# Seven half-size products in a sixth FFN tile too, weight sums made in two other tiles, last batch's plain q copied by DMA

## The chip, the core and the metric

The kernel runs on one core of one Trainium2 chip. The metric is the device time of one execution in microseconds (us), taken as the median of several runs. The engines are named as in the profile: PE is TensorE's matmuls, PEld its weight loads, DVE is VectorE, ACT is ScalarE, POOL is GpSimd, and SP is SyncE, whose queue issues DMAs.

## What is computed

Attention over 8 batches of 576 tokens with 8 heads of 64, then a feed-forward layer on the 4608 tokens of 512 that come out:

```
scores = q @ k^T / 8,  masked:
    heads 0 to 3 (plain):    0 <= i - j < 32
    heads 4 to 7 (dilated):  0 <= i - j < 128 and (i - j) % 4 == 0
x   = softmax(scores) @ v            # (8, 576, 8 x 64) -> (4608, 512)
h   = max(x @ w_in, 0)               # (4608, 2048)
out = (h * h) @ w_out                # (4608, 512), float32
```

Matrix products are in bfloat16 and accumulate in float32 in PSUM.

## The kernel before, in words

**Tiles and groups.** The feed-forward layer goes over nine tiles of 512 tokens, counted from one in this document (the first two tiles are worked on as four halves). Each tile is a list of 32 groups of instructions, so the n-th tile has the groups 32(n-1) to 32(n-1)+31. The first 16 are its first layer: group u multiplies x by 128 columns of w_in into one PSUM bank `pf` (L986, 4 matmuls of 512 columns), ScalarE takes the maximum with zero into `h2T` (L999), and VectorE squares it there (L1002). The other 16 are the second layer.

**The second layer, plain** (`g2`, L1157; tiles one to six). For each of four blocks of 128 tokens, 16 matmuls of 512 columns add into one bank (L1165), four in each group; ScalarE copies the bank to `osb` (L1171), and SP's queue stores it (L950).

**The second layer by seven products** (`g2_fast`, L1111; tiles seven to nine, `fast`, from `FAST * NT` tokens on). The 2048 inner rows are cut into two halves, the tokens of the tile into two halves, and the 512 output columns into two halves. Instead of eight products of half size, seven are made (M1 to M7, table `PRODUCTS` at L1093), each of 16 matmuls with 256 columns: 8 values of f times 2 blocks of tokens i. They need sums of the parts of h (`add_up`, L1032, four VectorE operations for a range of f, into `h_sum`, which lies in the staging buffers `rb[2]`, and in place in `h2T`) and sums of the parts of w_out (`weigh`, L1263, eight VectorE operations of 128x1024, into `w_sum`, which lies in `rb[0]`). The four quarters of the result, c11, c12, c21 and c22, lie in one buffer `whole`; `after` (L1057) copies a bank into a quarter on ScalarE or adds a bank to one on VectorE (`plus`, L1049), and `keep` (L1052) stores. In these tiles two f's that belong together are squared by one operation of 1024 elements, except the last two. f=0 to 7 (the low half) come from the even u, f=8 to 15 from the odd u. `sums_at` (L1024) says after which u the sums are made: 7, 11 and 15. Where an attention visit follows the first layer (`visited`, only the seventh tile), two of the last four sums are put off to a step of their own, "Z0".

Order before: M1 into bank X, M5 into Y, M6 on top of M1 in X, M3 on top of M5 in Y, M7 on top in X, M2 into Z, M4 on top in X. `after` reads the bank between the products that grow in it.

**The attention around it.** The attention of batch b (0 to 7) is spread over the groups as steps: (group number, order within a group, batch, code). `natural_step` (L696) carries one out after the group with that number is issued:

- "V": a visit (`quadrants`, L381): TensorE makes the scores of up to two heads' pairs e of a batch and the weighted sums of two others, all 64x64 quadrant matmuls (L376). Scores go to two banks `pa`, or to two banks `pf` for a second pair; sums and denominators to `po` and `pd`, and to two `pf` for a second pair.
- "E": exponential on ScalarE (L742), mask on VectorE (L747) and small sums there (L750, L759). A code with "e" makes only the exponentials, one with "m" only the masks.
- "L" and "X": the logarithm of the denominator (L709, L710), its exponential (L724) on ScalarE, and two multiplications on VectorE (L727, and L731 for 16 tokens whose values stand in a bank `pa`) that write x.
- "R", "K", "Q": `arrange` (L333) copies the transposed q and k of a batch into the layouts that the visits read (L352 and L355 for R, L346 for K, L344 for Q), mostly on VectorE.

From the sixth batch (b = 5) on, batch b has visits behind the groups 32(b-1)+15 and 32(b-1)+23, that is, between the first and second layer of tile b, counted from one, and in the middle of its second layer. In the sixth tile the first visit is that of b = 6; the second one makes scores of b = 7 and sums of b = 6. R of batch 7 stands at the groups 167 to 170, K at 170 to 172 and 184 to 187, Q at 173 to 175 and 188 to 191. In the third tile, R of batch 4 stands at the groups 82 to 85, and a visit behind group 88.

**What sets the order.** The program is written in the order in which each engine is to run it; every engine takes its own instructions strictly in that order, and waits are put in where two engines use the same tile. The main loop is:

```
    for g, group in enumerate(groups):
        ...
        group()
        if G * (FAST - 1) < g <= G * (FAST - 1) + 8:
            weigh(g - G * (FAST - 1) - 1)
        ...
        while steps and steps[0][0] <= g:
            natural_step(*steps.pop(0)[2:])
```

So before, the eight `weigh` operations stand behind the groups 161 to 168, in the sixth tile's first layer; a `weigh` stands ahead of the steps of its group. PSUM banks `pf` are four, given out in turn; `pa` are two; `po` and `pd` one each.

Of the kernel before, what the change touches and what calls it, by code (L numbers as in the profile page):

```python
# [63 lines left out]
def kernel(  # L64
# [9 lines left out]
    nc = tc.nc  # L74
    P = nc.NUM_PARTITIONS
    B, H, S, D = q.shape
# [17 lines left out]
    NT = 512  # L94
    NTILES = NTOK // NT
    XB = 2
    FAST = 6
    PAIRED = 5
    STAGE = (0, 1, 0, 2, 1, 1, 1, 1)
    NATURAL = 3  # L100
# [232 lines left out]
    def arrange(b: int, what: str, g: int, jj: int, e=None, copy=nc.vector.tensor_copy):  # L333

        src, rows = sides[jj], sides[g]
        n = H // 2
        hs = slice(0, n) if e is None else slice(2 * e, 2 * e + 2)  # L340
        if what == "Q" and b == XB:
            copy(qT[rows, 0:2, jj::2, :], qx[b % 2][src, g:4:2, :, :])
        elif what == "Q":
            copy(q_both[rows, hs, jj::2, :], qx[b % 2][src, hs, :, :])  # L344
        elif what == "K":
            nc.vector.tensor_copy(  # L346
                k_both[rows, g::2, hs, :].rearrange("p i h (c j m) -> p j (h c) i m", c=2, j=2)[:, jj, :, :, :],
                kx[b % 2][src, hs, :, :].rearrange("p h c (i m) -> p (h c) i m", m=16)[:, :, g::2, :],
            )
        else:  # L350
            ms = (slice(128, M), slice(0, 16))[g]
            copy(  # L352
                ends[b % 2][rows, 0, :, :].rearrange("p h (r m) -> p h r m", r=RES)[:, :, jj::2, :], qx[b % 2][src, n:, :, ms]
            )
            copy(  # L355
                ends[b % 2][rows, 1, :, :].rearrange("p h (m c j) -> p j h c m", c=2, j=2)[:, jj, :, :, :],
                kx[b % 2][src, n:, :, ms],
            )
# [337 lines left out]
    def natural_step(b: int, code: str):  # L696
        what, e = code[0], int(code[1])
        if what == "Z":
            late.pop()()
        elif what in "QKR":  # L700
            arrange(b, what, e, int(code[2]), *(int(x) for x in code[3:4]), *[nc.scalar.copy][: len(code) - 4])
        elif what == "V":
            scs, pvs = ([(int(x[0]), int(x[1])) for x in y.split(",") if x] for y in code[2:].split("/"))
            quadrants(scs, pvs)
        elif what == "L":
            _, d, rest = op[b, e]
            rec = recs[b, e] = r_pool.tile([P, 576], f32, name="rec")
            if rest[0][0] is rest[0][1]:
                nc.scalar.activation(rec[:, 0:512], d[:, :], ACT.Ln)  # L709
                nc.scalar.activation(rec[:, 512:576], rest[1][0], ACT.Ln)  # L710
            elif rest[0][0] is not rest[1][0]:
                nc.scalar.activation(rec[:, 0:512], d[:, :], ACT.Ln)
                for g in range(2):
                    to = sides[g ^ crossed(b, e)]
                    nc.scalar.activation(rec[to, 512:576], rest[1][g][to, :], ACT.Ln)
            else:
                for g in range(2):
                    to, at = sides[g], sides[1 - g]
                    nc.scalar.activation(rec[to, 512:576], rest[1][g][at, :], ACT.Ln)
                    nc.scalar.activation(rec[to, 0:512], d[at, :], ACT.Ln)  # L720
        elif what == "X":
            o, _, rest = op.pop((b, e))
            rec = recs.pop((b, e))
            nc.scalar.activation(rec[:, :], rec[:, :], ACT.Exp, scale=-1.0)  # L724
            t0 = b * M % (RING // RES)
            tok = xT[:, e, :, t0 : t0 + M]
            nc.vector.tensor_tensor(out=tok[:, :, 16:M], in0=byr(o[:, :]), in1=byr(rec[:, 0:512]), op=ALU.mult)  # L727
            for g, rows in enumerate(sides) if rest[0][0] is not rest[0][1] else [(0, slice(0, P))]:
                if rest[0][0] is not rest[1][0]:
                    g = g ^ crossed(b, e)  # L730
                nc.vector.tensor_tensor(  # L731
                    out=tok[rows, :, 0:16], in0=byr(rest[0][g][rows, :]), in1=byr(rec[rows, 512:576]), op=ALU.mult
                )
        else:
            g = int(code[2])
            second = g ^ ((b, e) in ((NATURAL, 1), (B - 1, 1)))
            n = 384 if e >= NE // 2 else (448, 384)[g]
            if "m" not in code:
                if not second:
                    pts[b, e] = p_pool.tile([P, 896], bf16, name="pt")  # L740
                pt = pts[b, e][:, 448 * g : 448 * g + n]
                nc.scalar.activation(pt, sp[b, e][g][:, 0:n], ACT.Exp, scale=SCALE)  # L742
            if "e" in code:
                return
            pt = pts[b, e][:, 448 * g : 448 * g + n]
            mask = (mask_f if e >= NE // 2 else mask_p[:, 384:] if b == XB else mask_n)[:, 0:n]
            nc.vector.tensor_tensor(out=pt, in0=pt, in1=mask, op=ALU.mult)  # L747
            if second and e >= NE // 2 and b > XB:
                z = pts[b, e][:, :].rearrange("p (x y) -> p x y", x=2)[:, :, 0:320].rearrange("p x (c m) -> p x c m", c=2)
                nc.vector.tensor_tensor(  # L750
                    out=shared[:, e - NE // 2], in0=z[:, :, :, 48:80], in1=z[:, :, :, 80:112], op=ALU.add
                )
            if second and e < NE // 2:
                even, odd = (
                    pts[b, e][:, y : y + 384].rearrange("p (i r m) -> p i r m", i=4, r=RES) for y in (0, 448)
                )
                for x, one, two in ((0, even, odd), (1, odd[:, 0:3], even[:, 1:4])):
                    n = 4 - x
                    nc.vector.tensor_tensor(  # L759
                        out=sums[:, e, 128 * x : 128 * x + 32 * n].rearrange("p (i r m) -> p i r m", i=n, r=RES),  # L760
                        in0=one[:, :, :, 16:24], in1=two[:, :, :, 0:8], op=ALU.add,
                    )
# [189 lines left out]
    def ffn_groups(tk0: int, nt: int):  # L952
# [69 lines left out]
                    late.append(lambda: add_up(*sums_at[u], (1, 3)))  # L1022

        sums_at = {7: (0, 4), 11: (4, 6), 15: (6, 8)}  # L1024
        visited = tk0 == FAST * NT

        def quarter(f0, f1, high, j):

# [28 lines left out]
        def after(name):  # L1057

            bank = {k: t[:, :, :] for k, t in cur.items()}
            if name == "M1":  # L1060
                nc.scalar.copy(c11, bank["X"])
            elif name == "M5":
                nc.scalar.copy(c22, bank["Y"])
            elif name == "M6":
# [5 lines left out]
            elif name == "M7":  # L1070
                plus(c22, bank["X"], c22)
                if final:
                    keep(1, HD, DM)
            elif name == "M2":
                plus(c11, bank["Z"], c11)
                keep(0, 0, DM)
            elif name == "M4":
                nc.scalar.copy(c21, bank["X"])
                keep(1, 0, HD if final else DM, by=nc.scalar if final else nc.sync)
# [10 lines left out]
        def w_of(x):  # L1090
# [8 lines left out]
            "M2": ("Z", raw(1, 0), w_raw(1, 0)),  # L1099
            "M4": ("X", raw(1, 1), w_of(3)),  # L1100
        }
        ITEMS = [(name, f, i, 0, HD) for name in PRODUCTS for f in range(NF // 2) for i in range(2)]
        if final:
            last = ITEMS[-NF:]
            one, *two_ = (
# [4 lines left out]

        def g2_fast(n):  # L1111

            head_ = 4 * NF
            lo, hi = (8 * n, 8 * n + 8) if n < 8 else (head_ + 6 * n - 48, head_ + 6 * n - 42 if n < 15 else len(ITEMS))
            if n == 0:
                for bank in "YX":
                    cur[bank] = ps_f.tile([P, 2, HD], f32, name="pf")
            for name, f, i, y0, y1 in ITEMS[lo:hi]:
                bank, lhs, rhs = PRODUCTS[name]
# [3 lines left out]
                if bank not in cur:  # L1123
                    cur[bank] = ps_f.tile([P, 2, HD], f32, name="pf")
                nc.tensor.matmul(  # L1125
                    cur[bank][:, i, y0:y1], lhs(f, i), rhs(f)[:, y0:y1],
                    start=f == 0 and (piece or name in ("M1", "M5", "M2") and i == 0), stop=f == NF // 2 - 1, skip_group_check=True,
                )
                if f < NF // 2 - 1:
                    continue  # L1130
# [219 lines left out]
    for b in range(NATURAL, B):  # L1350
# [35 lines left out]
            norm(1, t + 25)  # L1386
        else:
            visit(t + 15, [(b, 3), (b, 1)], [(b, 0), (b, 2)][: 1 + (b >= PAIRED)])
            if after:
                steps.extend((t + 15, 3, b, f"E1{x}") for x in range(2))  # L1390
            else:
                steps.extend((t + 15, 3, b, f"E1{x}e") for x in (1, 0))
# [1 line left out]
                steps.append((t + 16, 2, b, "Z0"))  # L1394
            if b >= PAIRED:
                norm(2, t + 15)
            expo(3, *[t + 17 - after] * 2)
            norm(0, t + 19 - 2 * after)
            visit(t + 23, [(b + 1, 2), (b + 1, 0)] if after else [], [(b, 1), (b, 3)])
            if after:  # L1400
                steps.extend((t + 23, 3, b + 1, f"E0{x}") for x in range(2))
                steps.extend((t + 27 + 2 * x, 1, b + 1, f"E2{x}") for x in range(2))
            norm(3, t + 23)
            norm(1, t + 25 - after)
        at = t - (14 if b < PAIRED else 19 if b == PAIRED else 25)
        for x, code in enumerate(("R00", "R01", "R10", "R11")):
            steps.append((start + 3 + x // 2 if early else at + x, 1, b, code))
# [13 lines left out]
    for g, group in enumerate(groups):  # L1421
# [6 lines left out]
                    load_qk(b + 1, part, [0, 1, 2, 3])  # L1428
            load_v_rows(b, "01")
        group()  # L1430
        if G * (FAST - 1) < g <= G * (FAST - 1) + 8:
            weigh(g - G * (FAST - 1) - 1)
        for code in program[g + 1] if g + 1 < len(program) else ():
            run(code)
        while steps and steps[0][0] <= g:
# [31 lines left out]
```

## Time and profile before

| | |
|---|---|
| median of 3 runs | 291.74 us (291.34 to 291.80) |
| the profiled execution | 293.39 us, its span from first to last instruction 291.6 us |
| TensorE clock granted, mean | 0.998 |
| sixth tile | 177.13 to 207.35 us |
| its first layer | 13.81 us |
| seventh tile (seven products) | 207.35 to 235.60 us |
| eighth tile (seven products, no attention) | 235.60 to 261.64 us |

The span is the time between the first and the last instruction in the trace; the rest of an execution's time lies around it. The profile's chain of waits follows the work that ended last back through the trace; a row of it has the start, the length, the engine, the tile written, the line and the number of instructions. A row of a timeline has the start, the busy time, the engine, the line, the operation, output and input, shapes and count; at its end, in brackets, stands how long the engine was idle before it and what released it. Where operations of an engine overlap in its pipeline, their rows overlap too, and the distance of two starts tells what one costs the engine.

### The profile page before, as it was taken

To read this page: it belongs to the slowest core of one execution; us is meant where nothing else is said; L and a number is where in the kernel's file an instruction comes from. 1 tells how busy PE (TensorE), PEld (TensorE's weight loads), DVE (VectorE), ACT (ScalarE), POOL (GpSimd) and SP (SyncE) were. 2 spreads that over 40 slices of the span, in tenths; PEclk is the share of its full clock that TensorE was granted. 3 is DMA by queue.
4 is the path that set the end of the run, shared out by engine and by line. 5 is a ranking of instruction groups with operands and counts; after the bars stand their busy time and mean duration, and the time that the engine had idled before them with its cause. 6 is when DMAs were issued, how large, how long until landed. Compare 5 with 4: busy or idle time off the path is not lost.

```text
span 291.6 us, 8217 instructions
## 1 busy us (share of the span) xinstructions
PE 285.7 (98%) x3377; PEld 180.4 (62%) x3377; DVE 178.4 (61%) x485; ACT 187.7 (64%) x381; POOL 122.8 (42%) x208
## 2 busy tenths in 40 slices
PE   8999999999999999999999999999999999999994
PEld 7679845958755554554555555555557865885684
DVE  1587414555869764688648747985469537623932
ACT  6588725787847855887757775667568646406620
POOL 8677266666272793767496379600000000000000
PEclk9999999999999999999999999999999999999999
DMA  7999999999999989999899999602100030002004
GB/s 116 193 187 212 204 202 202 183 151 172 133 162 218 176 109 221 149 163 136 124 164 203 115 138 200 81 2 74 72 1 2 2 146 0 2 32 112 2 0 144
DMA packets 83924, 35.77 MB, mean 123 GB/s; under 512 B 53168, under 2 KB 79280, under 8 KB 83888
## 3 DMA queue, kind: packets, MB, share of 16 engines
q0 software_dynamic: 49056, 18.49, 58.6%
q1 hardware_dynamic: 34416, 16.41, 26.8%
q8 instruction: 26, 0.43, 0.6%
q10 hardware_dynamic: 416, 0.36, 0.4%
q14 instruction: 10, 0.08, 0.1%
HBM read 37.50 MB, written 9.44 MB: 161 GB/s over the span
## 4 chain that ended last, share of the span: by engine, by line
PE 93%; ACT 2%; DVE 2%; DMA 1%; issue 1%; POOL 0%; POOLq 0%
PE pf L986 43%; PE pf L1165 26%; PE pf L1125 13%; PE po L376 2%; PE pa L376 1%; PE pf L376 1%; DMA kb<-in_k_dram 1%; PE pa L810 1%; PE po L780 1%; PE pd L376 1%; ACT pt L742 1%; ACT rec L724 0%; DVE xT L727 0%; PE pf L840 0%; PE pf L862 0%
## 5 line engine op out<-in xcount | busy, mean ns | idle before, releaser
L986 PE MATMUL pf<-xT,w_in 128*128 128x512 bf16 (+1 forms) x704 | 127.9, 341 | 0.4 <-DVE xT L934 0.3
L986 PEld LDWEIGHTS <-w_in 128*128 128x128 bf16 x704 | 78.2, 114 | 46.2 <-issue 0.9
L999 ACT ACTIVATE h2T<-pf 128x512 bf16<-128x512 f32 x143 | 83.9, 600 | 32.3 <-PE pf L986 32.1
L1165 PE MATMUL pf<-w_out_sb,h2T 128*128 128x512 bf16 x384 | 85.6, 379 | 0.1
L1002 DVE TENSOR_TENSOR h2T<-h2T 128x512 bf16<-128x512 bf16 (+1 forms) x123 | 55.8, 467 | 37.1 <-ACT h2T L999 35.5
L1165 PEld LDWEIGHTS <-h2T 128*128 128x128 bf16 x384 | 36.5, 98 | 42.3
L328 POOL DMA_DIRECT2D vbd<-in_v_dram x80 | 43.3, 567 | 25.3 <-DMA kb<-in_k_dram 13.2
L1171 ACT COPY osb<-pf 128x512 f32<-128x512 f32 x22 | 12.8, 583 | 20.7 <-PE pf L1165 20.7
L1125 PEld LDWEIGHTS <-h2T 128*128 128x128 bf16 x200 | 18.8, 98 | 2.6
L724 ACT ACTIVATE rec<-rec 128x576 f32<-128x576 f32 x24 | 16.4, 682 | 0.7
L182 POOL DMA_DIRECT2D qb<-in_q_dram x19 | 13.7, 722 | 6.2 <-DMA xx<-qb 4.2
L182 POOL DMA_DIRECT2D kb<-in_k_dram x19 | 13.3, 701 | 5.4 <-DMA w_out_sb<-in_moe_w_out_dram 1.7
L204 POOL DMA_DIRECT2D vbd<-in_v_dram x16 | 10.9, 685 | 10.6 <-DMA kb<-in_k_dram 6.1
L1050 DVE TENSOR_TENSOR whole<-pf,whole 128x512 f32<-128x512 f32 (+2 forms) x11 | 6.5, 594 | 13.9 <-PE pf L1125 13.9
L320 POOL DMA_DIRECT2D vbd<-in_v_dram x20 | 12.0, 616 | 7.2 <-DMA vbd<-in_v_dram 4.1
L742 ACT ACTIVATE pt<-pa 128x384 bf16<-128x384 f32 (+1 forms) x26 | 11.7, 498 | 4.9 <-DVE xT L731 4.2
L314 POOL DMA_DIRECT2D vd<-in_v_dram x20 | 12.0, 614 | 3.7 <-DMA vbd<-in_v_dram 2.4
L727 DVE TENSOR_TENSOR xT<-pf,rec 128x512 bf16<-128x512 f32 x11 | 7.6, 690 | 8.2 <-ACT rec L724 8.2
L727 DVE TENSOR_TENSOR xT<-po,rec 128x512 bf16<-128x512 f32 x13 | 9.0, 690 | 5.8 <-ACT rec L724 5.6
L747 DVE TENSOR_TENSOR pt<-pt,mask_f 128x384 bf16<-128x384 bf16 x24 | 8.3, 353 | 5.8 <-ACT pt L742 5.7
L1125 PE MATMUL pf<-w_out_sb,h2T 128*128 128x256 bf16 (+1 forms) x104 | 11.7, 264 | 0.0
L1125 PE MATMUL pf<-kb,h2T 128*128 128x256 bf16 x96 | 11.5, 273 | 0.0
(176 smaller groups left out, 381.1 us busy)
## 6 DMA issues: line engine op xcount, KB each, us to landing
out_dram<-osb SPq DMA_DIRECT2D x24, 128.0 KB, 4.9
out_dram<-osb SPq DMA_DIRECT2D x12, 256.0 KB, 4.3
qb<-in_q_dram POOLq DMA_DIRECT2D x7, 320.0 KB, 9.2
kb<-in_k_dram POOLq DMA_DIRECT2D x7, 320.0 KB, 9.3
vd<-in_v_dram POOLq DMA_DIRECT2D x34, 64.0 KB, 5.0
w_out_sb<-in_moe_w_out_dram POOLq DMA_DIRECT2D x4, 512.0 KB, 13.6
out_dram<-whole SPq DMA_DIRECT2D x4, 512.0 KB, 3.1
qb<-in_q_dram POOLq DMA_DIRECT2D x6, 256.0 KB, 6.4
```

The lines of the kernel that those rows point to most:

```text
L182: nc.gpsimd.dma_start(t[p0 : p0 + n, part, h0:h1, :], src[b, h0:h1, t0 : t0 + RES * n, :].rearrange("h (p r) d -> p h (r d)", r=RES),)
L328: nc.gpsimd.dma_start(v_rows[b % 2][p0 + 16 * r : p0 + 16 * r + 16, e, :, :], v[b, 2 * e + hl, :, :].rearrange("(i m r) d -> r m i d", r=R ...
L376: nc.tensor.matmul(out, lhs, rhs, start=begin, stop=True, skip_group_check=True)
L724: nc.scalar.activation(rec[:, :], rec[:, :], ACT.Exp, scale=-1.0)
L727: nc.vector.tensor_tensor(out=tok[:, :, 16:M], in0=byr(o[:, :]), in1=byr(rec[:, 0:512]), op=ALU.mult)
L742: nc.scalar.activation(pt, sp[b, e][g][:, 0:n], ACT.Exp, scale=SCALE)
L986: nc.tensor.matmul(to, w_in_sb[piece][:, kt, c0 : c0 + 509 : 4], rhs, start=(kt == kts[0] and x == 0), stop=(kt == kts[-1] and x == per - ...
L999: nc.scalar.activation(hv, acc[u][:, :].rearrange("p (x n) -> p x n", x=per), ACT.Relu)
L1002: nc.vector.tensor_tensor(out=hv, in0=hv, in1=hv, op=ALU.mult)
L1125: nc.tensor.matmul(cur[bank][:, i, y0:y1], lhs(f, i), rhs(f)[:, y0:y1], start=f == 0 and (piece or name in ("M1", "M5", "M2") and i == 0), ...
L1165: nc.tensor.matmul(cur[m][:, c0:c1], h2[:, f, P * m : P * m + P], w_out_sb[:, f, c0:c1], start=(f == 0), stop=(f == NF - 1),)
L1171: (nc.vector.tensor_copy if last and part == 1 or tk0 == 3 * NT // 2 else nc.scalar.copy)(osb[:, c0:c1], cur[m][:, c0:c1])
```

## The change

- `FAST` goes from 6 to 5, so that the sixth tile makes its second layer by seven products too, with squares in pairs and sums of h. `visited` now holds for the sixth and the seventh tile; a new name, `crowded`, for the sixth alone.
- In the sixth tile the products go in another order and into other banks: M1 into X, the first block of M2 into Z, M6 on top of M1 in X, the second block of M2, M5 on top in X; then, behind the second visit, M7 into V, M3 into Q, and M4 on top of M7 in V. ScalarE copies X into c11, c21 and c12 after M1, M6 and M5; VectorE adds: c11 gets Z, c22 is V plus c12, c12 gets Q, c21 gets V. Two stores of 512 KB each follow M3 and M4.
- The eight `weigh` operations stand behind the groups 84, 86, 88, 90 (third tile, second layer) and 130, 132, 134, 136 (fifth tile, first layer).
- Q of the last batch (b = 7), eight copies, is done by DMAs that SP issues in place of VectorE's copies.
- Batch 6 gets the step order that only batch 7 had: its E1 exponentials for both halves first, the masks a group later together with "Z0", E3 at group 177 instead of 176, L0 at 179 instead of 177. Behind the second visit of the sixth tile L3 and L1 come first and X3 and X1 one group later than before.

```diff
-    FAST = 6
+    FAST = 5
+    WEIGH = (84, 86, 88, 90, 130, 132, 134, 136)
...
-        if what == "Q" and b == XB:
+        if what == "Q" and b == B - 1:
+            nc.sync.dma_start(q_both[rows, hs, jj::2, :], qx[b % 2][src, hs, :, :])
+        elif what == "Q" and b == XB:
...
-            second = g ^ ((b, e) in ((NATURAL, 1), (B - 1, 1)))
+            second = g ^ ((b, e) in ((NATURAL, 1), (B - 2, 1), (B - 1, 1)))
...
-        visited = tk0 == FAST * NT
+        visited, crowded = FAST * NT <= tk0 <= (FAST + 1) * NT, tk0 == FAST * NT
...
+            elif crowded and name in ("M6", "M5"):
+                nc.scalar.copy(c21 if name == "M6" else c12, bank["X"])
+            elif crowded and name != "M2":
+                to, one, two_ = {"M7": (c22, "V", c12), "M3": (c12, "Q", c12), "M4": (c21, "V", c21)}[name]
+                plus(to, bank[one], two_)
+                if name != "M7":
+                    keep(int(name == "M4"), 0, DM)
...
-                keep(0, 0, DM)
+                if not crowded:
+                    keep(0, 0, DM)
...
+        fresh, CUTS = "M1 M5 M2", [8 * n if n < 8 else 6 * n + 16 for n in range(NF)]
         ITEMS = [(name, f, i, 0, HD) for name in PRODUCTS for f in range(NF // 2) for i in range(2)]
+        if crowded:
+            for name, bank in (("M5", "X"), ("M7", "V"), ("M3", "Q"), ("M4", "V")):
+                PRODUCTS[name] = bank, *PRODUCTS[name][1:]
+            fresh, CUTS = "M1 M2 M7 M3", [8 * n if n < 10 else 6 * n + 20 - max(0, n - 12) for n in range(NF)]
+            ITEMS = [
+                (name, f, i, 0, HD)
+                for name, only in (("M1", None), ("M2", 0), ("M6", None), ("M2", 1), ("M5", None), ("M7", None), ("M3", None), ("M4", None))
+                for f in range(NF // 2)
+                for i in range(2)
+                if only in (None, i)
+            ]
...
-            head_ = 4 * NF
-            lo, hi = (8 * n, 8 * n + 8) if n < 8 else (head_ + 6 * n - 48, head_ + 6 * n - 42 if n < 15 else len(ITEMS))
+            lo, hi = (CUTS + [len(ITEMS)])[n : n + 2]
             if n == 0:
-                for bank in "YX":
+                for bank in "ZX" if crowded else "YX":
...
-                    start=f == 0 and (piece or name in ("M1", "M5", "M2") and i == 0), stop=f == NF // 2 - 1, skip_group_check=True,
+                    start=f == 0 and (piece or name in fresh and i == 0), stop=f == NF // 2 - 1, skip_group_check=True,
...
-            if after:
+            quick = b > FAST
+            if not quick:
                 steps.extend((t + 15, 3, b, f"E1{x}") for x in range(2))
...
-            expo(3, *[t + 17 - after] * 2)
-            norm(0, t + 19 - 2 * after)
+            expo(3, *[t + 16 + quick] * 2)
+            norm(0, t + 17 + 2 * quick)
...
-            norm(3, t + 23)
-            norm(1, t + 25 - after)
+            if quick and after:
+                steps.extend([(t + 23, 3, b, "L3"), (t + 24, 3, b, "L1"), (t + 25, 0, b, "X3"), (t + 26, 0, b, "X1")])
+            else:
+                norm(3, t + 23)
+                norm(1, t + 25 - after)
...
-        if G * (FAST - 1) < g <= G * (FAST - 1) + 8:
-            weigh(g - G * (FAST - 1) - 1)
+        if g in WEIGH:
+            weigh(WEIGH.index(g))
```

## The prediction

> **What bounds the kernel now.** I read the page first, then the chain of waits, then the timelines of VectorE and ScalarE around the stages that the diff touches. Tiles are counted from one, so the sixth tile starts at group 160; M1 to M7 are the seven products.
>
> ```profile
> span 291.6 us, 8217 instructions
> PE 285.7 (98%) x3377; PEld 180.4 (62%) x3377; DVE 178.4 (61%) x485; ACT 187.7 (64%) x381; POOL 122.8 (42%) x208
> PE 93%; ACT 2%; DVE 2%; DMA 1%; issue 1%; POOL 0%; POOLq 0%
> PE pa L376 <- DVE kbd L355: 0.3, 1, 0.3
> ```
>
> TensorE is busy 98% of the span and is 93% of the chain. So a matmul that goes is worth its whole spacing, and a wait that comes is paid whole: TensorE has no later idle time of any size to take it up. In the middle of the kernel one matmul wait is listed, the fourth line: one visit of the attention waits 0.3 us for VectorE.
>
> The stages in the chain (start us, length, matmuls):
>
> ```profile
> 109.80 0.22 PE pa L376 x3
> 177.13 13.81 PE pf L986 x64
> 192.14 7.01 PE pf L1165 x32
> 199.15 0.15 PE po L376
> 200.34 7.01 PE pf L1165 x32
> 207.35 13.81 PE pf L986 x64
> 222.36 7.09 PE pf L1125 x64
> 230.24 5.37 PE pf L1125 x48
> 249.41 12.23 PE pf L1125 x112
> ```
>
> The sixth tile runs from 177.13 to 207.35. Its plain second layer is the two pieces of 7.01, 14.02 us for 64 matmuls of 512 columns, with a visit of 200.34 - 199.15 = 1.19 us between them. The seventh tile, with seven products and visits of its own, needs 7.09 + 5.37 = 12.46 for 112 matmuls of 256 columns; the eighth, without attention, 12.23.
>
> **The change, part by part.** *Seven products in the sixth tile.* Unhindered, they save 14.02 - 12.46 = 1.56 us (1.79 at the eighth tile's rate). I take 1.56, since the seventh tile also has visits.
>
> *The weights' sums.* Eight subtractions of 128x1024 leave the sixth tile; four go to groups 84 to 90 and four to 130 to 136. What one costs VectorE is seen where it stands between squares:
>
> ```profile
> 183.28 0.41 DVE L1002 TENSOR_TENSOR h2T<-h2T 128x512 bf16<-128x512 bf16 x1
> 183.62 0.68 DVE L1275 TENSOR_TENSOR qb<-w_out_sb,qb 128x1024 bf16<-128x1024 bf16 x1
> 184.22 0.42 DVE L1002 TENSOR_TENSOR h2T<-h2T 128x512 bf16<-128x512 bf16 x1
> ```
>
> From start to start 184.22 - 183.62 = 0.60 us; a square of 512 takes 0.34 in the same way. In the third tile:
>
> ```profile
> 107.62 0.38 DVE L352 COPY kbd<-xx 64x128 bf16<-64x128 bf16 x1
> 108.86 0.24 DVE L352 COPY kbd<-xx 64x128 bf16<-64x128 bf16 x1
> 109.39 0.36 DVE L355 COPY kbd<-xx 64x128 bf16<-64x128 bf16 x1
> 111.02 0.69 DVE L727 TENSOR_TENSOR xT<-po,rec 128x512 bf16<-128x512 f32 x1 [1.28 <-ACT rec L724]
> 117.22 0.36 DVE L747 TENSOR_TENSOR pt<-pt,mask_f 128x384 bf16<-128x384 bf16 x1 [2.41 <-ACT pt L742]
> ```
>
> These are the four end codes of the fifth batch (R00 to R11, steps 82 to 85), two copies each, back to back; the last ends at 109.75 and the visit behind group 88 goes on at 109.80. Group 84's subtraction is emitted before step 84, so it stands in VectorE's queue ahead of R10. R11 then ends 0.60 later, and the visit waits 0.34 + 0.60. That is **+0.60** on the path, bounds 0.5 to 0.7. The subtraction of 86 comes behind R11; those of 88 and 90 come ahead of two normalizations (the first at 111.02) and the key and query copies. They push those back by about 1.2 us, which the idle 2.41 before 117.22 takes up. In the fifth tile:
>
> ```profile
> 153.57 0.43 DVE L1002 TENSOR_TENSOR h2T<-h2T 128x512 bf16<-128x512 bf16 x1 [0.44 <-ACT h2T L999]
> 167.39 0.21 DVE L731 TENSOR_TENSOR xT<-pa,rec 128x64 bf16<-128x64 f32 x1
> 168.89 0.15 PE po L376
> ```
>
> There 0.44 us lies idle before each square up to 154.4, so three subtractions fit. The fourth (group 136) makes all behind it about 0.7 late; the normalization that ends at 167.60 then ends at 168.3, still ahead of the visit at 168.89. Cost 0; without that margin it would be 0.7.
>
> *VectorE in the sixth tile's first layer.* It loses the subtractions and four query copies, squares in pairs, and gains the sums of h. The seventh tile shows this work already, but without the next batch's R and key copies, which the sixth must do as well:
>
> ```profile
> 214.92 0.69 DVE L1002 TENSOR_TENSOR h2T<-h2T 128x1024 bf16<-128x1024 bf16 x1 [1.03 <-ACT h2T L999]
> 221.23 1.35 DVE L1002 TENSOR_TENSOR h2T<-h2T 128x1024 bf16<-128x1024 bf16 x3
> 223.08 0.43 DVE L1043 TENSOR_TENSOR qb<-qb,h2T 128x512 bf16<-128x512 bf16 x1
> 223.97 0.69 DVE L727 TENSOR_TENSOR xT<-pf,rec 128x512 bf16<-128x512 f32 x1 [0.47 <-ACT rec L724]
> 224.58 0.21 DVE L731 TENSOR_TENSOR xT<-pa,rec 128x64 bf16<-128x64 f32 x1
> ```
>
> From 214.92 on VectorE doesn't pause there until the last sum, which starts at 223.08; some 0.35 later, at 223.43, it could take the next operation (the normalization of 223.97 waits for ScalarE). All R and key copies of the sixth tile (steps 167 to 172) fall into that stretch, so their time X is added in full. In the trace of before:
>
> ```profile
> 186.09 0.18 DVE L352 COPY kbd<-xx 64x128 bf16<-64x128 bf16 x1
> 186.33 0.41 DVE L1002 TENSOR_TENSOR h2T<-h2T 128x512 bf16<-128x512 bf16 x1
> 188.72 0.43 DVE L1002 TENSOR_TENSOR h2T<-h2T 128x512 bf16<-128x512 bf16 x1
> 189.18 0.19 DVE L352 COPY kbd<-xx 64x128 bf16<-64x128 bf16 x1
> 191.77 0.29 DVE L344 COPY qT<-xx 64x576 bf16<-64x576 bf16 x1
> ```
>
> From 186.09 to 191.77 are 5.68 us: the four R pairs, four key copies, one subtraction with a copy behind it (0.68), and six squares, two at 0.34 and four at 0.46, since a square with a copy behind it takes 189.18 - 188.72. So R and keys take 5.68 - 0.68 - 2.52 = 2.48. Three new changes from arithmetic to copies (0.08 to 0.12 each) make **X = 2.75**. Bounds: 1.0 (four times the shortest pair, 186.33 - 186.09, and nothing for the keys) and 3.4 (pairs as in the third tile, 109.75 - 107.62 = 2.13, with 0.95 for keys and 0.3).
>
> Now the seventh tile's rows 30.22 us earlier (207.35 - 177.13), plus X. The pair square that makes f=6 starts at 221.23 - 30.22 + 2.75 = 193.76, ends at 194.45, and TensorE sees it at 194.50. M1 starts at 192.14, 0.1108 a matmul (7.09/64), and its thirteenth needs f=6 at 193.47: a wait of 1.03. The single square of f=7 is 0.34 behind while two matmuls take 0.22: 0.12 more. **M1's wait: 1.15.**
>
> M1, M6 and M5 grow in one bank, and ScalarE copies it out after each; eight matmuls of M2 (0.89) stand between. A free ScalarE does the copy in 0.58 (third row below), so M6 finds its bank read. Before M5 it isn't free:
>
> ```profile
> 195.68 0.87 ACT L742 ACTIVATE pt<-pa 128x384 bf16<-128x384 f32 x2 [1.97 <-DVE xT L731]
> 197.19 0.68 ACT L724 ACTIVATE rec<-rec 128x576 f32<-128x576 f32 x1
> 224.25 0.58 ACT L1061 COPY whole<-pf 128x512 f32<-128x512 f32 x1 [0.31 <-PE pf L1125]
> ```
>
> E3's two exponentials (first row) wait for VectorE's small normalization out of the same bank pa, though both only read. The new c21 copy comes in group 180, behind E3 (step 177) and L0 (179), 197.19 - 195.68 = 1.51 after E3's start. VectorE is free for this normalization's first half at 223.43 - 30.22 + 2.75 = 195.96 and ends the small one 0.82 later (224.58 + 0.21 - 223.97), at 196.78. So E3 starts at 196.81, the copy runs 198.32 to 198.90, and TensorE goes on at 198.95. M1, M2, M6, M2 end at 192.14 + 48 x 0.1108 + 1.15 = 198.61. **M5's wait: 0.34**, whatever X is, once M1 waits.
>
> The Trainium skill, "PSUM — Partial Sum Buffer", section "PSUM bank collisions raise a hardware error", says that two engines must not use one bank and partition quadrant at once, reads included, so that accesses have to be ordered by bank. The 1.97 us agrees; without such an order M5 would not wait and the sum would be 0.34 less.
>
> M5 ends at 200.72 and the visit runs to 201.91. What it needs from VectorE (X0, M2's addition into c11, E3's masks) is done by my count 0.1 to 0.4 before its use: cost 0, up to 0.3 if not. The last 48 matmuls take 5.37, to 207.28; the additions for M7, M3 and M4 lie beside them, and M4 finds its bank read since M3's 16 matmuls lie between. **The sixth tile gains 207.35 - 207.28 = 0.07 us** of its 1.56.
>
> *Query copies of the last batch by DMA.* Eight issues move to SP. For the first four (steps 173 to 175):
>
> ```profile
> 177.37 30.96 SPq L950 DMA_DIRECT2D out_dram<-osb  x10
> qb<-in_q_dram POOLq DMA_DIRECT2D x7, 320.0 KB, 9.2
> 186.59 1.08 POOL L328 DMA_DIRECT2D vbd<-in_v_dram  x2 [0.59 <-DMA vbd<-in_v_dram]
> ```
>
> SP has only the fifth tile's last stores ahead of them. Issued by 191 and landing as slowly as a 320 KB load (9.2), they are there at the visit of 200.7. The other four stand behind the store that waits for M3's addition, and are needed 14 us later. Cost 0; late landing would cost its lateness.
>
> The last row shows GpSimd done at 187.67, and X's copies come from 188.1 on. In the third tile, where the pairs took 2.13 us, GpSimd was issuing throughout. The Trainium skill, "SBUF — State Buffer", section "Who interferes with whom", says that a VectorE copy in a two-port mode and GpSimd lock each other out; by that rule the dear end of X has no ground here and the sum keeps 2.75. The sum itself doesn't use it.
>
> **Sum.** +0.60 - 0.07 = +0.53. The profiled execution took 293.39 us, its span 291.6 and 1.8 around it; the median of the runs is 291.74. A shift inside the span carries over: **292.3 us**.
>
> **The rivals.** *Faster:* VectorE keeps pace. From X = 1.7 down neither wait is there, and -1.56 + 0.60 gives 290.8. For it: the shortest pair four times leaves 0.7 for the keys, and the seventh tile's M1 doesn't wait. Against: the 2.48 measured on these same copies. *Slower:* the copies are dear. Above X = 2.8 the sixth tile gains nothing and each us of X is a us of M1's wait; at 3.4 it is +1.2, 292.9. For it: the third tile's pairs; against: the pairs of 187 to 189. *The subtraction costs nothing in the third tile*, if the visit's 0.34 has another cause than R11: 291.7. Against: the copy's end and the visit differ by 0.05. That the query DMAs are late has 10 us against it and gets no chance of its own.
>
> **How the numbers follow.** Forecast 0.55 (its own range 291.9 to 292.7), faster rival 0.20, slower rival 0.17, third 0.08. A measurement of this kernel can tell about 0.2% (0.58 us) from no change, which is 292.32, in the middle of the forecast's range: 0.28 of its chance counts as same, 0.27 as slower. Faster 0.20, same 0.28 + 0.08 = 0.36, slower 0.27 + 0.17 = 0.44. The range goes from just above the faster rival, 290.9, to just above the slower one, 293.0.
>
> **What would show it.** Right: the visit behind group 88 waits about 0.9 us for L355; M1 of the sixth tile has about 1.1 us of idle before f=6 and f=7, with the pair square as releaser; M5 waits some 0.3 us for a ScalarE copy. Wrong: no idle in M1 (X is small), an E3 that doesn't wait for VectorE, or a visit in the sixth tile that waits.

## The result and the profile after

| | before | after |
|---|---|---|
| median, runs of this comparison | 291.77 us (291.34 to 291.84, 4 runs) | 293.09 us (292.94 to 293.29, 4 runs) |
| ratio | | 1.0049, 95% interval 1.0031 to 1.0066 |
| profiled execution, its span | 293.39, 291.6 us | 292.94, 291.1 us |

In this comparison the change made the kernel slower by 1.3 us. The forecast was 292.3 us with a range up to 293.0, so the measured median lies 0.1 us outside. In e2, e6 and e11 below, one execution each was 1.8 to 3.2% longer at a lower granted clock (0.971 to 0.992), and the medians given here leave it out. The profiled execution of the changed kernel is nevertheless shorter than the one of before; the reason is at its beginning, and it matters for how far a trace may be set against a median. From the page and the waits of TensorE after the change:

```profile
span 291.1 us, 8310 instructions
PE 281.1 (97%) x3411; PEld 183.7 (63%) x3425; DVE 182.3 (63%) x486; ACT 186.9 (64%) x380; POOL 122.9 (42%) x208
L1187 PE MATMUL pf<-w_out_sb,h2T 128*128 128x512 bf16 x306 | 70.0, 379 | 1.2 <-issue 0.6
L1187 PEld LDWEIGHTS <-h2T 128*128 128x128 bf16 x320 | 30.4, 98 | 35.1
PE pf L1147 <- DVE h2T L1005: 1.0, 1, 1.0
PE pa L379 <- DVE kbd L358: 0.7, 1, 0.7
```

Line numbers have moved: L1187 is the matmul of the plain second layer, L1147 that of the seven products, L1005 the square, L358 the second copy of an R pair, L379 a visit's matmul. The busy time listed for TensorE is 4.6 us less than before, but that is not what was saved: 14 of the 320 plain matmuls have no record in this trace (306 against 320 weight loads), some 3 us at 7.01/32 = 0.219 each. Two waits stand out: the one in the seven products that was not there, and the visit's wait for L358, 0.7 where it was 0.3. The chain of waits after the change gives the stages:

```profile
146.27 13.81 PE pf L989 x64
...
176.52 6.92 PE pf L989 x32
...
201.36 5.34 PE pf L1147 x48
206.71 13.81 PE pf L989 x64
...
229.59 5.37 PE pf L1147 x48
234.96 13.81 PE pf L989 x64
```

The sixth tile runs from 176.52 to 206.71: 30.19 us, against 30.22 before. The fifth (30.25) and the seventh (28.25) are as they were, 30.27 and 28.25. So seven products brought 0.03 us net in the one tile that they were put in.

Where the sixth tile's 1.6 us went is seen in three timelines of it. TensorE, the matmuls of the seven products up to the second visit:

```profile
191.46 1.49 PE L1147 MATMUL pf<-w_out_sb,h2T 128*128 128x256 bf16 x12
193.97 1.60 PE L1147 MATMUL pf<-w_out_sb,h2T 128*128 128x256 bf16 x12 [1.02 <-DVE h2T L1005]
195.40 1.91 PE L1147 MATMUL pf<-qb,qb 128*128 128x256 bf16 x16
197.15 1.04 PE L1147 MATMUL pf<-w_out_sb,h2T 128*128 128x256 bf16 x8
198.27 1.91 PE L1147 MATMUL pf<-qb,qb 128*128 128x256 bf16 x16
```

The starts tell the waits. Twelve matmuls at 12.23/112 = 0.109 take 1.31, so the thirteenth was due at 192.77 and came at 193.97: 1.20. The next twelve took 195.40 - 193.97 = 1.43, 0.12 too long (f=7). M6's 16 took 1.75, as they should. M2's second eight should take 0.87, and M5 came 1.12 after them: 0.25. VectorE and ScalarE at these places:

```profile
192.47 0.71 DVE L349 COPY kbd<-xx 64x320 bf16<-64x320 bf16 x3
193.22 1.36 DVE L1005 TENSOR_TENSOR h2T<-h2T 128x1024 bf16<-128x1024 bf16 x3
195.41 0.68 DVE L730 TENSOR_TENSOR xT<-pf,rec 128x512 bf16<-128x512 f32 x1
196.01 0.21 DVE L734 TENSOR_TENSOR xT<-pa,rec 128x64 bf16<-128x64 f32 x1
```

```profile
196.26 0.87 ACT L745 ACTIVATE pt<-pa 128x384 bf16<-128x384 f32 x2 [0.94 <-DVE xT L734]
197.60 0.62 ACT L1066 COPY whole<-pf 128x512 f32<-128x512 f32 x1
```

VectorE comes from the key copies without a pause to the three squares (f=6 with f=14, then f=7, then f=15), and TensorE goes on at 193.97, when the first of them is done. ScalarE's E3 waits 0.94 for the small normalization L734, and the copy of bank X stands behind it; TensorE goes on at 198.27, 0.05 after the copy's end.

### The profile page after: what moved, and what is told of

The parts are those of the page before. It is cut to its first block, busy times and chain, and to the rows that moved or that the text cites. A ratio compares the mean times of both kernels' runs of the same rounds, so it can differ in the third digit from the quotient of the medians.

```text
span 291.1 us, 8310 instructions
## 1 busy us (share of the span) xinstructions
PE 281.1 (97%) x3411; PEld 183.7 (63%) x3425; DVE 182.3 (63%) x486; ACT 186.9 (64%) x380; POOL 122.9 (42%) x208
## 4 chain that ended last, share of the span: by engine, by line
PE 56%; DMA 28%; POOL 6%; DVE 4%; issue 3%; ACT 1%; POOLq 0%; DVEq 0%
PE pf L989 26%; PE pf L1147 15%; DMA kb<-in_k_dram 14%; PE pf L1187 12%; DMA w_out_sb<-in_moe_w_out_dram 4%; DMA qb<-in_q_dram 3%; DMA vd<-in_v_dram 3%; DMA w_in<-in_moe_w_in_dram 2%; DMA vbd<-in_v_dram 2%; POOL qb L183 1%; DVE h2T L1005 1%; POOL kb L183 1%; PE po L379 1%; DVE qb L1046 1%; POOL vd L232 1%
## 5 line engine op out<-in xcount | busy, mean ns | idle before, releaser
L1005 DVE TENSOR_TENSOR h2T<-h2T 128x512 bf16<-128x512 bf16 (+1 forms) x116 | 54.5, 486 | 37.0 <-ACT h2T L1002 35.3
L1187 PE MATMUL pf<-w_out_sb,h2T 128*128 128x512 bf16 x306 | 70.0, 379 | 1.2 <-issue 0.6
L1187 PEld LDWEIGHTS <-h2T 128*128 128x128 bf16 x320 | 30.4, 98 | 35.1
L1147 PEld LDWEIGHTS <-h2T 128*128 128x128 bf16 x264 | 24.7, 98 | 4.9 <-DVE h2T L1005 1.5
L1193 ACT COPY osb<-pf 128x512 f32<-128x512 f32 x18 | 10.5, 584 | 17.0 <-PE pf L1187 17.0
L1053 DVE TENSOR_TENSOR whole<-pf,whole 128x512 f32<-128x512 f32 (+2 forms) x15 | 9.3, 618 | 14.6 <-PE pf L1147 13.8
L1147 PE MATMUL pf<-w_out_sb,h2T 128*128 128x256 bf16 (+1 forms) x136 | 15.8, 267 | 1.0 <-DVE h2T L1005 1.0
L1147 PE MATMUL pf<-kb,h2T 128*128 128x256 bf16 x128 | 15.3, 273 | 0.0
L1147 PE MATMUL pf<-qb,qb 128*128 128x256 bf16 x128 | 14.8, 273 | 0.1
L1147 PEld LDWEIGHTS <-qb 128*128 128x128 bf16 x128 | 12.5, 98 | 1.7 <-issue 0.3
```

Of the source, the lines that this page charges most:

```text
L1005: nc.vector.tensor_tensor(out=hv, in0=hv, in1=hv, op=ALU.mult)
L1147: nc.tensor.matmul(cur[bank][:, i, y0:y1], lhs(f, i), rhs(f)[:, y0:y1], start=f == 0 and (piece or name in fresh and i == 0), stop=f == NF ...
L1187: nc.tensor.matmul(cur[m][:, c0:c1], h2[:, f, P * m : P * m + P], w_out_sb[:, f, c0:c1], start=(f == 0), stop=(f == NF - 1),)
```

## The experiments

Each run has its own profile; the "sixth tile" and the "third tile" are counted from the first first-layer matmul of the tile to that of the next one, and "wait" is TensorE's at the visit behind group 88. "Third to ninth" is the time from the first first-layer matmul of the third tile to that of the ninth, which holds both places that the theory is about. All of it is from TensorE's timelines and waits; e5, e7 and e8 were timed in one execution each, so only their traces are used.

| run | profiled execution | first first-layer matmul at | wait | third tile | sixth tile | third to ninth |
|---|---|---|---|---|---|---|
| before, as first profiled | 293.39 | 16.28 | 0.34 | 31.36 | 30.22 | 176.83 |
| e1_before_again | 294.39 | 15.89 | 0.39 | 31.41 | 30.22 | 176.83 |
| e9_before_third | 291.47 | 14.64 | 0 | 31.08 | 30.22 | 176.50 |
| after | 292.94 | 15.19 | 0.69 | 31.71 | 30.19 | 177.12 |
| e2_after_again | 292.80 | 14.61 | 1.01 | 32.10 | 30.19 | 177.55 |
| e10_after_third | 292.57 | 14.44 | 1.08 | 32.10 | 30.19 | 177.51 |
| e3_weights_only | 293.89 | 14.64 | 0.91 | 31.92 | 30.22 | 177.45 |
| e4_weights_late | 291.91 | 14.41 | 0.16 | 31.18 | 30.20 | 176.62 |
| e5_no_copies | 290.74 | 14.96 | 0.07 | 31.11 | 28.63 | 174.98 |
| e6_gpsimd_copies | 290.06 | 14.39 | 0.09 | 31.11 | 28.63 | 174.96 |
| e7_query_copies_back | 293.12 | 14.67 | 0 | 31.00 | 31.62 | 177.90 |
| e8_e3_behind_copy | 292.73 | 14.15 | 0.23 | 31.25 | 31.44 | 177.93 |
| e11_gpsimd_again | 290.24 | 14.65 | 0.07 | 31.08 | 28.63 | 174.92 |
| e12_gpsimd_early_weights | 291.44 | 14.56 | 1.04 | 32.05 | 28.63 | 175.89 |

**The theory** (A) is the prediction's: one subtraction ahead of R10 lengthens the wait of the visit behind group 88, and the sixth tile gives back its saving in two waits, both set by VectorE's copies of the last batch. Rivals were that the loss lies in the sixth tile alone, or ahead of all this, in the first 16 us.

**The same kernels again, and the weights' sums alone.** First, before and after were run once more, with two kernels that differ in where the subtractions stand.

> The kernel before, unchanged, run as a candidate against itself. Theory A (the profiled execution of before, 293.39 us, was a long one of its kernel, by about 1.6 us, all of it in the first 16 us): ratio 1.000 within 0.002, a span of about 290.0 us in its profile instead of 291.6, the first-layer matmuls starting at about 14.7 us instead of 16.28, and the same stage lengths from there on. Theory B (profiled executions of this kernel are 1.6 us longer than timed ones): ratio 1.000 and a span of 291.6 again.

> The changed kernel, unchanged, on the same chip as the others of this batch. Theory A: ratio 1.0045 again, and its sixth tile again 30.2 us long. If the difference belongs to a chip or a moment and not to the program, the ratio moves towards 1.000.

In the third kernel only the place of the subtractions is taken over from the change:

```diff
+    WEIGH = (84, 86, 88, 90, 130, 132, 134, 136)
-        if G * (FAST - 1) < g <= G * (FAST - 1) + 8:
-            weigh(g - G * (FAST - 1) - 1)
+        if g in WEIGH:
+            weigh(WEIGH.index(g))
```

> Before, with only the weights' sums moved to groups 84 to 90 and 130 to 136; seven products still only from the seventh tile on. Theory A (the subtraction ahead of R10 makes the visit behind group 88 wait 0.6 us longer, nothing else does): +0.6 us, ratio 1.002. Rival (the extra 1.3 us come from the sixth tile alone): 0.0 us. Rival (they come from what stands ahead of 16 us and differs with any rebuilt program): anything, with the head of the trace showing it.

In the fourth, the changed kernel has the first four two groups later:

```diff
-    WEIGH = (84, 86, 88, 90, 130, 132, 134, 136)
+    WEIGH = (86, 88, 90, 92, 130, 132, 134, 136)
```

> The changed kernel with the first four subtractions at groups 86, 88, 90 and 92 instead of 84, 86, 88 and 90, so that none stands ahead of R10 and R11. Theory A: 0.6 us less than the changed kernel (about 292.5), and the visit behind group 88 waits 0.3 us or less. Rival (the visit waits for something else than R11): the same time as the changed kernel.

Measured: before against itself 292.30 us, ratio 1.0031 (1.0002 to 1.0059); after 292.80, 1.0033 (1.0009 to 1.0057); weights only 292.47, 1.0016 (0.9995 to 1.0037); weights late 291.95, 1.0008 (0.9985 to 1.0031); before in the same batch 291.79. So the profiled execution of before was a long one again (theory A's 290.0 us of span was not met here, only later, by e9, whose profiled execution lies 0.2 us below its median; that speaks against theory B). Nor is all that executions differ by at the head: between the first first-layer matmul and the third tile e1 takes 69.75 us and e3 69.89, where the others take 68.4 to 68.9. And two timings of one program came out 0.3% apart: e1's ratio is as high as e2's, and e2's median is only 0.5 us above e1's. The times alone decide little at this size; the waits do. TensorE's waits for the R copy, from the changed kernel (e2), weights only (e3) and weights late (e4):

```profile
PE pa L379 <- DVE kbd L358: 1.0, 1, 1.0
```

```profile
PE pa L377 <- DVE kbd L356: 1.3, 2, 0.9
```

```profile
PE pa L379 <- DVE kbd L358: 0.2, 1, 0.2
```

With the subtraction ahead of R10 the visit waits 0.9 to 1.0 here (0.7 in the first trace of the changed kernel), whatever the sixth tile does; two groups later it waits 0.2. The rival that the loss is the sixth tile's alone falls, and so does the one that the visit waits for something else than R11.

**The sixth tile's two waits.** The next four kernels start from the one with the late subtractions. In the first, the twelve copies that make up X are left out:

```diff
+        if b == B - 1 and (what == "R" or what == "K" and e == 0):
+            return
```

> The changed kernel with the later subtractions, and the R copies and the first four key copies of the last batch left out (that batch's scores are made from what lies there). Theory A (M1 waits for the square behind these copies, M5 for a ScalarE copy that stands behind VectorE's normalization): X is 0, both waits go, and the sixth tile's length in the trace falls from 30.19 to about 28.7 us. Rival (M1 waits for ScalarE or for its own pipeline): it stays at 30.2.

In the second, GpSimd makes them:

```diff
+        if b == B - 1 and (what == "R" or what == "K" and e == 0):
+            copy = nc.gpsimd.tensor_copy
...
-            nc.vector.tensor_copy(
+            copy(
```

> The changed kernel with the later subtractions, and those twelve copies made by GpSimd, which has nothing to do from about 187.7 us on. Theory A: the same 28.7 us for the sixth tile as without the copies, if GpSimd is done by the visit at 199; 1.4 us less than before, ratio 0.995. Rival (the copies on GpSimd slow VectorE's operations beside them, or end too late): the sixth tile between 29 and 30.2, with the visit or VectorE's rows showing which.

In the third, the last batch's queries are copied by VectorE as before the change:

```diff
-        if what == "Q" and b == B - 1:
-            nc.sync.dma_start(q_both[rows, hs, jj::2, :], qx[b % 2][src, hs, :, :])
-        elif what == "Q" and b == XB:
+        if what == "Q" and b == XB:
```

> The changed kernel with the later subtractions and the last batch's query copies on VectorE again instead of DMAs. Theory A: one copy (0.3) stands ahead of the square of f=7 and all four ahead of the normalization that E3 waits for: M1 waits 0.3 longer and M5 0.9 longer, the sixth tile takes 31.4 us. Rival (the DMAs bring nothing, VectorE has room): 30.2.

In the fourth, E3, L0 and X0 of batch 6 come later:

```diff
-            expo(3, *[t + 16 + quick] * 2)
-            norm(0, t + 17 + 2 * quick)
+            late_e3 = 3 * (quick and after)
+            expo(3, *[t + 16 + quick + late_e3] * 2)
+            norm(0, t + 17 + 2 * quick + late_e3 // 2)
```

> The changed kernel with the later subtractions, E3's exponentials moved from step 177 to 180, behind the c21 copy in ScalarE's queue, and L0 and X0 to 180 and 181. Theory A: M5 no longer waits (0.34 less), but E3's masks and X0 come after the second visit's start and it waits 0.7 to 1.0: the sixth tile takes 30.5 to 30.9 us, the wait has only moved. Rival (M5 waits for something else than the copy behind E3): M5's idle stays.

Measured, sixth tile: 28.63, 28.63, 31.62 and 31.44 us. Without the copies on VectorE both waits are gone, 30.20 - 28.63 = 1.57 us. The chain of e6 through the sixth tile has no wait in it, and GpSimd's row shows that the copies end at 189.69, well ahead of the visit at 197.3:

```profile
190.20 7.09 PE pf L1149 x64
198.48 5.35 PE pf L1149 x48
```

```profile
187.42 2.27 POOL L351 COPY kbd<-xx 64x320 bf16<-64x320 bf16 x4
```

With the query copies back on VectorE, M1 and M5 wait longer. TensorE's rows of e7:

```profile
190.24 1.48 PE L1145 MATMUL pf<-w_out_sb,h2T 128*128 128x256 bf16 x12
192.74 0.39 PE L1145 MATMUL pf<-w_out_sb,h2T 128*128 128x256 bf16 x2 [1.01 <-DVE h2T L1003]
193.28 1.27 PE L1145 MATMUL pf<-w_out_sb,h2T 128*128 128x256 bf16 x10 [0.15 <-DVE h2T L1003]
194.39 1.91 PE L1145 MATMUL pf<-qb,qb 128*128 128x256 bf16 x16
196.13 1.04 PE L1145 MATMUL pf<-w_out_sb,h2T 128*128 128x256 bf16 x8
198.49 1.91 PE L1145 MATMUL pf<-qb,qb 128*128 128x256 bf16 x16 [1.32 <-ACT whole L1064]
```

Counted by the starts as above, the first 24 matmuls take 4.15 in place of 3.94, so M1 waits 0.2 longer (0.3 expected). The last row is M5's wait for the c21 copy: it comes 2.36 after M2's second half begins, a wait of 1.49 in place of the 0.25 above, 1.2 longer (0.9 expected). The four copies stand ahead of the normalization that E3 waits for, and the whole row of waiting engines moves. So in the changed kernel the DMAs do bring 31.62 - 30.20 = 1.4 us. With E3 behind the copy (e8), M5 has no wait (its row starts 0.87 after M2's second half), and the visit has one:

```profile
195.69 1.04 PE L1147 MATMUL pf<-w_out_sb,h2T 128*128 128x256 bf16 x8
196.56 1.91 PE L1147 MATMUL pf<-qb,qb 128*128 128x256 bf16 x16
199.44 0.42 PE L379 MATMUL po<-pt,vbd 64*64 64x96 bf16 x2 [0.97 <-DVE xT L734]
```

That is the wait moved, as expected, but dearer: 31.44 against the 30.5 to 30.9 expected. M5's 16 matmuls take 16 x 0.109 = 1.75, so the visit begins at 196.56 + 1.75 = 198.31, and the next product, M7, starts at 201.09: the visit with its waits takes 2.8 us instead of 1.2.

**What the change costs in all, and the better version.** The last four were run together, to set before and after against each other with profiles of executions that are alike at the beginning.

> The kernel before as a candidate once more, as a measure of what two timings of one program differ by. Theory A: the stages from the fourth tile on as in every trace of it so far (30.69, 30.27, 30.22, 28.25, 26.04); the wait of the visit behind group 88 between 0 and 0.4 us; what the executions differ by lies ahead of the first first-layer matmul (14.1 to 16.3 us so far). Ratio 1.000 within 0.003.

> The changed kernel as a candidate once more, on the same chip as the row above. Theory A (the change costs the 0.7 us of one subtraction at the visit behind group 88 and nothing else): that visit waits 0.7 to 1.0 us, the sixth tile takes 30.19, and the median is 0.7 us above that of the row above. Rival (there is a further cost of 0.5 us outside these two places): the median is 1.2 us or more above it, and a stage or the head of the trace is longer by that.

> The version with later subtractions and the twelve copies on GpSimd, a second time and on another chip. Theory A: the sixth tile 28.63 again, 1.6 us less than the kernel before in the sixth tile, ratio 0.995 within 0.002.

> The same with the first four subtractions back at 84, 86, 88 and 90. Theory A: the sixth tile stays at 28.63, the visit behind group 88 waits 0.7 us longer, and the median is 0.7 us above the row above. Rival (the subtraction's place is of no account once the sixth tile is free): the same median.

Measured: e9 291.68, ratio 0.9991 (0.9968 to 1.0014); e10 292.80, 1.0031 (1.0004 to 1.0058); e11 290.83, 0.9971 (0.9951 to 0.9992); e12 291.00, 0.9983 (0.9961 to 1.0004); before 291.92. The traces of e9 and e10 begin alike (14.64 and 14.44) and differ mainly in one stage: the third tile, 31.08 and 32.10. VectorE's R copies there, e9 first:

```profile
106.05 0.19 DVE L352 COPY kbd<-xx 64x128 bf16<-64x128 bf16 x1
107.54 0.30 DVE L355 COPY kbd<-xx 64x128 bf16<-64x128 bf16 x1
```

```profile
106.03 0.19 DVE L355 COPY kbd<-xx 64x128 bf16<-64x128 bf16 x1
106.14 0.53 DVE L358 COPY kbd<-xx 64x128 bf16<-64x128 bf16 x1
106.80 0.43 DVE L358 COPY kbd<-xx 64x128 bf16<-64x128 bf16 x1
107.26 0.69 DVE L1297 TENSOR_TENSOR qb<-w_out_sb 128x1024 bf16<-128x1024 bf16 x1
107.96 0.19 DVE L355 COPY kbd<-xx 64x128 bf16<-64x128 bf16 x1
108.49 0.30 DVE L358 COPY kbd<-xx 64x128 bf16<-64x128 bf16 x1
```

And the visit's last scores, again e9 first:

```profile
107.69 0.43 PE L376 MATMUL pa<-kbd 64*64 64x64 bf16 x4
```

```profile
108.85 0.22 PE L379 MATMUL pa<-kbd 64*64 64x64 bf16 x3 [1.08 <-DVE kbd L358]
```

In e9 R11 ends at 107.84 and the scores go through without a listed wait. In e10 the subtraction takes 107.96 - 107.26 = 0.70 from start to start, not 0.60; two of the copies are longer as well, and R11 ends at 108.79. In the expectation of e10 the rival asked for 1.2 us and a stage that shows it: the medians differ by 1.12, and 1.02 of it stands in the third tile, at the very place of the theory.

Not all of the 1.02 is the subtraction's. In the five traces that have it ahead of R10 it takes 0.70 or 0.71. The eight R copies without it take 1.7 to 2.1 us in these five and 1.7 to 2.2 in the other nine, so they vary by themselves, whichever kernel it is: 108.79 - 106.03 - 0.70 = 2.06 in e10 and 107.84 - 106.05 = 1.79 in e9.

The wait without the subtraction ahead of R10 is 0.15 us in the mean of nine traces of the table, with it 0.95 in the mean of five. That is 0.80 us. Before against after alone, three traces each, the waits differ by 0.68 in the mean, and third to ninth by 0.67. e12 shows the same beside a free sixth tile: its visit waits 1.04, its third tile takes 32.05, its span is 1.2 us longer than e11's (289.6 and 288.4). The medians of e11 and e12, 290.83 and 291.00, hardly show it, and by the expectation's letter the rival has the medians and the theory the trace. What the other executions of the two look like inside is not on record; no run here separates that.

The version of e6 and e11 beats both kernels: 290.63 and 290.83 us, ratios to before 0.9953 (0.9927 to 0.9979) and 0.9971 (0.9951 to 0.9992). A ratio of 0.997 alone would not carry this, as e1 was off by as much; the traces do. Third to ninth takes 174.96 and 174.92, 1.5 to 1.9 less than in the three traces of before, as the sixth tile is 1.59 us shorter and the visit behind group 88 hardly waits.

## Why the prediction was wrong, point by point

- **The step that failed** is the size of the term "+0.60 on the path, bounds 0.5 to 0.7". The mechanism was right, the place too. The subtraction itself cost 0.70 or 0.71 there in all five traces that have it; the visit's wait grew by 0.80 in the mean of the table, and by more between e9 and e10, since the R copies were slower in e10. Two things were missed. The 0.60 was read where a square follows the subtraction; here a copy follows. The prediction took 0.68 for that very case in working out X, some paragraphs on, and not here. And it took the visit's wait before, 0.34, from one execution, as if it were fixed: in three traces of that kernel it is 0.34, 0.39 and 0, because the four R pairs take 2.13, 2.17 and 1.79 us. The prediction set the pairs' 2.13 beside GpSimd's issuing; in e11 GpSimd issued DMAs without a pause beside them too, and they took 1.70. What stretches them is not shown.
- **This step does not make up the whole miss.** With 0.80 for 0.60 and 0.03 for 0.07 the sum is 291.74 + 0.77 = 292.5, inside the range. The other 0.6 us of the measured 293.09 are not placed by any trace, except for 0.1 behind the last matmul (4.14 to 4.22 us from its start to the end of the span in the ten traces of kernels with `FAST` at 5, 4.06 to 4.09 in the other four). The prediction took 0.2% for what a measurement can tell from no change and gave the range no room for timing; two timings of the kernel before gave ratios to itself of 1.0031 and 0.9991, that is +0.9 and -0.3 us. Whether the rest is timing or a cost outside the traces stays open.
- **The sixth tile** was right: gain 0.07 forecast, 0.03 measured. Step by step, with the tile 0.61 us earlier than in the profile of before: the pair square of f=6 was forecast for 193.15 and started at 193.22; M1's wait 1.15, measured 1.20 + 0.12 = 1.32; the normalization 195.35, measured 195.41; M5's start 198.34, measured 198.27; its wait 0.34, measured 0.25. E3 waits for a VectorE read of the same bank again: 0.94 us after the change, and 2.18 in e7, where the normalization came later. The Trainium skill, "PSUM — Partial Sum Buffer", section "PSUM bank collisions raise a hardware error", says that two engines must not use one bank and partition quadrant at once, reads included. The order kept here agrees; no run leaves it out.
- **X = 2.75** was right to about 0.1: after the change the twelve copies take 0.86, 0.85, 0.15 and 0.75 us, in four stretches from the first copy's start to the next operation's, 2.61 in all. The two rivals about it fell: VectorE didn't keep pace, and the pairs were not dear in the sixth tile. e5 and e6 show what the faster rival would have been worth: 1.57 us.
- **The edits costed at nothing** were so: the fifth tile, with four more subtractions, takes 30.25 us against 30.27, the query DMAs delay no visit, and the last products start 1.75 us apart, without a wait.
- **The sum.** The traces show 0.80 - 0.03 = 0.77 us. The medians say 1.3, 1.0 and 0.9, or 0.5 and 1.1 against e1 and e9, the same kernel in the same two batches. The range's upper end, 293.0, was built from a dear X alone; the bounds of the failed term, at 0.7, were too narrow for what the profile's own R pairs (0.42 to 0.69 from start to start) could have told.

## What to carry to other kernels

When a bound engine gets less to do, price the engine that has to feed it at the same place: here seven eighths of the matmuls would have saved 1.6 us, and what stood in VectorE's queue ahead of the squares decided whether any of it arrived. Work that is moved "somewhere idle" has to be set against the next due time in that queue and not against the idle share of the stage: two groups later the same four subtractions were free. Take the cost of an operation from a row with the same neighbour behind it, and a wait from several executions before adding to it. And time the kernel against itself before reading a difference of 0.3%.

## What the runs showed of the hardware

- What a VectorE operation costs from start to start depends on what stands behind it: the subtraction 0.60 ahead of a square (before), and 0.70 ahead of R10's first copy (e10). A copy is not the reason by itself. In e10 a subtraction also costs 0.61 ahead of another one and 0.72 ahead of a normalization:

```profile
108.82 0.69 DVE L1297 TENSOR_TENSOR qb<-w_out_sb 128x1024 bf16<-128x1024 bf16 x1
109.43 0.69 DVE L1297 TENSOR_TENSOR kb<-w_out_sb 128x1024 bf16<-128x1024 bf16 x1
110.15 0.69 DVE L730 TENSOR_TENSOR xT<-po,rec 128x512 bf16<-128x512 f32 x1
```

In the sixth tile after the change a sum of 128x1024 with R00's first copy behind it costs 187.48 - 186.87 = 0.61. R00 writes the lower 64 partitions, where the sum's output begins too, and R10 the upper 64. That fits, but no run changes this alone.

- GpSimd makes the 64x320 copies in 2.27/4 = 0.57 us each (e6), where VectorE's three take 0.71/3 = 0.24 (after). VectorE's sums beside GpSimd's copies became longer. From e6:

```profile
187.76 0.55 DVE L1048 TENSOR_TENSOR qb<-h2T 128x512 bf16<-128x512 bf16 x1
191.28 0.42 DVE L1048 TENSOR_TENSOR qb<-h2T 128x512 bf16<-128x512 bf16 x1
```

The first runs while GpSimd copies, the second after it, 0.55 against 0.42. The Trainium skill, "SBUF — State Buffer", section "Who interferes with whom", says that a VectorE operation with two inputs in SBUF contends with a GpSimd instruction that reads SBUF; these rows agree. It cost nothing here: the sixth tile takes 28.63 us with these copies on GpSimd as without them (e6, e5).
